# Local and global attention followed by a gated MLP: the order of every engine laid out by a list scheduler in the kernel

## The chip, the cores and the metric

The kernel runs on one core of a Trainium2 chip. The time is device microseconds of that core for one execution, median of several runs. A core has five engines that run side by side, each through its own list of instructions in order: TensorE (PE in the profile; its weight loads are PEld), VectorE (DVE), ScalarE (ACT), GpSimd (POOL) and SyncE (SP). Here POOL issues all loads from memory, which convert fp32 to fp16 on the way, and SP issues the stores and the copies within the on-chip memory. All transfers share 16 DMA engines. An engine whose next instruction waits for something lets everything behind it wait too.

## The reference

There are 8 batches, 8 heads, 512 local and 32 global positions, and a head size of 64. A local query sees the local keys within 32 positions and all 32 global keys; a global query sees all 544 keys. The attention output then goes through two matrix products with a hard-swish between them.

```python
s_g = scale * q_g @ concat(k_g, k_l).T;  out_g = softmax(s_g) @ concat(v_g, v_l)
s_ll = where(|i - j| <= 32, scale * q_l @ k_l.T, -1e9)
s_l = concat(scale * q_l @ k_g.T, s_ll); out_l = softmax(s_l) @ concat(v_g, v_l)
x = concat(out_g, out_l) as 4352 rows (batch, position) of 512 (head, channel)
h = x @ w_in                      # 512 x 2048
g = h * clip(h + 3, 0, 6) / 6
out = g @ w_out                   # 2048 x 512
```

## The kernel before

**Attention of a batch.** `qk_loads` (L85 to L101) loads q and k of a batch as eight transfers of 128 positions by 8 heads by 64 channels, and for every second batch the global q and k of two batches (`qkg`). Four `pair_qk` (L180) turn two heads at a time: eight TensorE transposes into the one `t` buffer of PSUM, then one ACT copy to `qk` (L189). `global_qk` (L169) does it for `qkg`. `v_loads` (L103) loads V into overlapping windows of 96 keys, `spread` (L115) copies the global V beside each window by three DMAs, and `shift` (L121 to L124) makes the two copies of V shifted by 32 and 64 keys by four DMAs inside the on-chip memory; both go through SP.

The batch has six blocks: four local ones of 128 queries (`local_scores` L191, `turn` L220, `local_av` L229, `local_x` L251) and two global ones, for even and odd heads (`global_scores` L262, `turn`, `global_av` L294, then `global_x` L309). A local block is 64 small score matmuls (32 of L206 and 32 of L208), then for each of the 8 heads one DVE instruction that adds the mask and takes the maximum (L214) and one ACT exponential (L217), then 8 transposes (L223), an ACT copy to `et` (L225), 32 matmuls with V (L236), a normalisation on DVE (L248, L249), and a DMA transpose on SP that puts the result in `xt` (L255). PSUM has one buffer each for scores (`s`), transposes (`t`) and attention output (`a`), and three for the MLP (`m`).

**MLP of a batch.** `first` (L318) makes one of 16 slices of the hidden layer: four matmuls into an `m` buffer (L323), an ACT ReLU to `t1` (L327), and on DVE the gate (L328) that also frees the `m` buffer. `second` (L332) makes 128 rows of the output in four quarters of four matmuls (L338), a DVE copy (L342), and a store on SP (L355). In the first batch, `first` runs on two halves of 256 positions.

**What sets the order.** The loop over blocks (L423 on) runs a pipeline of three stages: scores of block i, transposes of block i-1, V matmuls of block i-2. Between the stages `fill` (L385) takes work from the list `pending` (the MLP of earlier batches), 4/3 pieces at a time. The framework then orders the instructions by that priority and by free buffers. The loads of batch b+1 are issued six at a time within the blocks of batch b. At the start POOL issues: q and k of batch 0, the identity, the global q and k, the mask, V, then `w_in` in four transfers and `w_out` in sixteen (L404 to L414); batch 1 follows.

The TensorE list that comes out is periodic from the second batch on. Per batch, with S for local and GS for global scores, T for transposes, A and GA for V matmuls, pair for q and k, F for `first`, W for `second`, and the number of matmuls behind each:

```text
W1 pair8 W5 pair8 W2 GS32 A32 W4 T6 W8 pair8 W5 pair8 W3 S64 GA24 W8 T6 W16 S64 GA24 W4 T8 W8 F8
S64 A32 F4 T8 F8 S6 F4 GX1 S17 F4 S41 A32 F8 T8 F4 GS6 F8 GS2 F4 GS24 A32 F4 T8 F8
```

## Time and profile before

| What | us |
|---|---|
| median of 3 runs (428.4 to 430.57) | 428.52 |
| the profiled execution, its own time | 429.63 |
| its span, first to last instruction | 427.8 |
| outside the span | 1.83 |
| PE busy | 360.1 (84%) |
| ACT busy | 243.5 (57%) |
| DVE busy | 221.2 (52%) |
| POOL busy | 119.6 (28%) |
| bytes moved by DMA | 44.54 MB |

A row of a timeline gives the start in microseconds, how long the merged run of instructions lasts, engine, line, operation, written and read tiles, and how many; in brackets how long the engine stood idle before it and what released it. A row of windows gives a stretch of time, its length, and for each engine its busy time and number of instructions, then the granted TensorE clock (1.00 is full), the DMA share and the rate in GB/s. A matmul's length includes its way through the array, so the pace of a run is read from start to start, not from the single durations.

### The profile page before, as it was taken

How to read it: one execution, taken by the hardware profiler on the slowest of the kernel's cores; microseconds unless marked ns; L12 is line 12 of the kernel's file. 1: busy time of each engine (PE TensorE's matmuls, PEld its weight loads, DVE VectorE, ACT ScalarE, POOL GpSimd, SP SyncE). 2: the span in 40 equal slices, each digit the busy share in tenths (PEclk: the TensorE clock that was granted, in tenths of full speed). 3: DMA queues.
4: the chain of work that ended last, by engine and by line, in shares of the span. 5: the costliest groups of instructions: out<-in, count | busy, mean ns of one | idle time of the engine just before them, and what ended most of it. 6: DMA issues, size and time to landing. Idle time of an engine off the chain costs nothing.

```text
span 427.8 us, 13784 instructions
## 1 busy us (share of the span) xinstructions
PE 360.1 (84%) x5784; PEld 205.1 (48%) x5784; DVE 221.2 (52%) x873; ACT 243.5 (57%) x533; POOL 119.6 (28%) x170
## 2 busy tenths in 40 slices
PE   0447059597999999999989999999999989999996
PEld 0325036365555455555545554555445544544642
DVE  2044015474348734873577357735773578437611
ACT  1456118675567756785677567856676667227500
POOL 8923697473642034203420252010000000000000
PEclk9999999888999999999999999999999999999999
DMA  9999999999999359945993698353602110120021
GB/s 94 107 207 201 141 152 181 141 178 152 112 190 150 41 76 182 157 44 75 183 158 36 82 174 163 33 85 89 136 12 52 52 41 14 51 75 0 2 74 74
DMA packets 140541, 44.54 MB, mean 104 GB/s; under 512 B 125888, under 2 KB 134592, under 8 KB 140480
## 3 DMA queue, kind: packets, MB, share of 16 engines
q0 software_dynamic: 111040, 17.57, 60.0%
q1 hardware_dynamic: 29440, 26.09, 26.9%
q8 instruction: 45, 0.74, 0.7%
q14 instruction: 16, 0.13, 0.1%
HBM read 35.13 MB, written 8.91 MB: 103 GB/s over the span
## 4 chain that ended last, share of the span: by engine, by line
PE 61%; ACT 14%; DMA 8%; issue 6%; POOL 5%; DVE 5%; POOLq 0%; ACTq 0%
PE m L338 27%; PE m L323 19%; ACT t L327 5%; ACT ex L217 5%; DMA win<-in_moe_w_in_dram 4%; DVE gt L328 4%; PE s L281 4%; PE t L186 3%; PE t L223 3%; PE a L236 2%; DMA wout<-in_moe_w_out_dram 2%; PE s L206 2%; ACT qk L189 2%; DMA qn<-in_q_l_dram 1%; POOL kn L101 1%
## 5 line engine op out<-in xcount | busy, mean ns | idle before, releaser
L323 PE MATMUL m<-xt,win 128*128 128x512 f16 (+1 forms) x576 | 129.4, 363 | 21.2 <-DVE gt L328 12.4
L338 PE MATMUL m<-wout,gt 128*128 128x512 f16 x512 | 123.1, 380 | 0.0
L328 DVE SCALAR_TENSOR_TENSOR gt<-t,m 128x512 f16<-128x512 f32 (+1 forms) x144 | 86.8, 625 | 45.4 <-ACT t L327 44.7
L327 ACT ACTIVATE t<-m 128x512 f32<-128x512 f32 (+1 forms) x160 | 82.0, 532 | 42.4 <-PE m L323 41.0
L217 ACT ACTIVATE ex<-sm,mx 128x128 f16<-128x128 f32 x256 | 78.7, 388 | 41.7 <-DVE mx L214 41.6
L323 PEld LDWEIGHTS <-win 128*128 128x128 f16 x640 | 59.5, 99 | 64.2 <-issue 18.7
L214 DVE CUSTOM_DVE_ANT_0 sm<-s,mask 128x128 f32<-128x128 f32 x256 | 57.0, 287 | 48.5 <-PE s L208 41.2
L338 PEld LDWEIGHTS <-gt 128*128 128x128 f16 x512 | 46.7, 98 | 46.2
L111 POOL DMA_DIRECT2D vw<-in_v_l_dram x48 | 35.6, 746 | 98.1 <-PE a L236 86.6
L189 ACT COPY qk<-t 128x1024 f16<-128x1024 f16 x32 | 32.6, 1018 | 49.2 <-PE t L186 49.0
L225 ACT COPY et<-t 128x1024 f16<-128x1024 f16 (+1 forms) x48 | 44.7, 930 | 12.7 <-PE t L223 12.6
L342 DVE COPY ot<-m 128x512 f32<-128x512 f32 x34 | 23.4, 688 | 46.7 <-PE m L338 46.7
L284 DVE TENSOR_REDUCE mx<-s 128x1 f32<-128x768 f32 x16 | 15.3, 958 | 39.7 <-PE s L281 39.7
L186 PE MATMUL t<-ident,qn 128*128 128x128 f16 x128 | 14.3, 233 | 23.2 <-POOL ident masks.py:199 9.6
L101 POOL DMA_DIRECT2D qn<-in_q_l_dram x32 | 29.1, 909 | 16.6 <-PE t L186 13.3
L101 POOL DMA_DIRECT2D kn<-in_k_l_dram x32 | 29.2, 911 | 0.6 <-DMA wout<-in_moe_w_out_dram 0.6
L186 PEld LDWEIGHTS <-qn 128*128 128x128 f16 x128 | 10.8, 104 | 36.7 <-DMA qn<-in_q_l_dram 18.3
L206 PEld LDWEIGHTS <-qk 64*32 64x32 f16 x1024 | 15.7, 90 | 23.8 <-issue 15.9
L206 PE MATMUL s<-gt,qk 64*32 64x32 f16 x1024 | 22.1, 185 | 5.8 <-issue 4.5
L223 PE MATMUL t<-ident,ex 128*128 128x128 f16 x256 | 24.4, 234 | 2.3 <-ACT ex L217 2.2
L236 PE MATMUL a<-vw,et 128*32 128x65 f16 x1024 | 17.0, 202 | 9.1 <-DMA vw<-vw 3.9
L208 PE MATMUL s<-qk 64*32 64x96 f16 x1024 | 23.5, 211 | 0.0
(53 smaller groups left out, 292.6 us busy)
## 6 DMA issues: line engine op xcount, KB each, us to landing
out_dram<-ot SPq DMA_DIRECT2D x32, 256.0 KB, 3.7
vw<-vw SPq DMA_DIRECT2D x16, 330.0 KB, 5.7
vw<-vgs SPq DMA_DIRECT2D x24, 198.0 KB, 4.7
qn<-in_q_l_dram POOLq DMA_DIRECT2D x32, 128.0 KB, 5.4
kn<-in_k_l_dram POOLq DMA_DIRECT2D x32, 128.0 KB, 5.6
vw<-in_v_l_dram POOLq DMA_DIRECT2D x32, 96.0 KB, 4.8
vw<-vw SPq DMA_DIRECT2D x16, 165.0 KB, 5.4
win<-in_moe_w_in_dram POOLq DMA_DIRECT2D x4, 512.0 KB, 15.7
```

What stands on the lines that cost most here:

```text
L101: return [lambda o=o, i=i: nc.gpsimd.dma_start(out=o, in_=i) for o, i in work]
L186: nc.tensor.matmul(out=ps[:, c0:c0 + P], lhsT=nat[:, j, p * P:(p + 1) * P], rhs=ident, is_transpose=True)
L189: nc.scalar.copy(out=dst, in_=ps.rearrange("d (i s) -> d i s", i=2))
L206: nc.tensor.matmul(out=o[:, 0:Sg], lhsT=lhs, rhs=st["gt"][rows, p, gc:gc + Sg])
L214: nc.vector.tensor_tensor_reduce(out=sm, in0=ps[:, h % 2, h // 2, :], in1=m, scale=-scale, scalar=3.0e38, op0=ALU.add, op1=ALU.min, accum_ ...
L217: nc.scalar.activation(out=ex[:, h, :], in_=sm, func=EXP, scale=-1.0, bias=mx)
L223: nc.tensor.matmul(out=ps[:, h * P:(h + 1) * P], lhsT=ex[:, h, :], rhs=ident, is_transpose=True)
L225: nc.scalar.copy(out=et[:, 0:n, :].rearrange("c h q -> c (h q)"), in_=ps)
L323: nc.tensor.matmul(out=ps[:, 0:n], lhsT=w_in_t[c // WC][:, m, c % WC * P:(c % WC + 1) * P], rhs=x[:, m, 0:n], start=(m == 0), stop=(m == N ...
L327: nc.scalar.activation(out=t1[:, 0:n], in_=ps[:, 0:n], func=RELU, bias=0.5, scale=1.0 / 6.0)
L328: nc.vector.scalar_tensor_tensor(out=g[:, 0:n], in0=t1[:, 0:n], scalar=1.0, in1=ps[:, 0:n], op0=ALU.min, op1=ALU.mult)
L338: nc.tensor.matmul(out=ps, lhsT=gs[c][:, t0:t0 + P], rhs=w_out_t[c], start=(c == 0), stop=(c == NDFF - 1))
```

## The change

**Order.** The loop over blocks, `fill` and `pending` are gone. Every piece of work is registered by `op(engine, t, cost, f, deps, ...)` with a priority time `t`, a cost in microseconds, the pieces it depends on and the buffers it takes and frees. `lay_out` replays the five engines and the queue of loads with these costs, picks at each step the ready piece with the smallest `t` on the engine that is free first, and so lists all pieces. They are then emitted in that order, and `tc.manual_schedule()` makes the framework keep it. The maximum and the exponential of each head are pieces of their own (`head_max`, `head_exp`), so that MLP work on ACT and DVE can stand between two heads.

```python
def lay_out():
    ...
    while len(order) < len(ops):
        best = None
        for e, line in avail.items():
            can = [(r, o) for o in line for r in (ready(o),) if r is not None]
            if not can:
                continue
            now = max(free[e], min(r for r, _ in can))
            o = min((o for r, o in can if r <= now), key=lambda o: o.t)
            if best is None or now < best[0]:
                best = (now, e, o)
        ...
        order.append(o)
...
with tc.manual_schedule():
    for o in lay_out():
        o.f()
```

**Loads.** For batches 0 and 1, q and k come as two transfers each of four heads, in which a partition holds four consecutive positions, so that 256 numbers (1 KB) are read in one piece instead of 64. `w_out` comes in four transfers instead of sixteen. POOL issues: global V, q and k of heads 0 to 3, identity, mask, global q and k, q and k of heads 4 to 7, V of batch 0, `w_in`, all of batch 1, `w_out`, then q and k of batch 2. The mask takes two POOL instructions instead of eight, and three DVE copies.

```diff
+        if b < LONG:
+            h = i // 2 * (H // 2)
+            load(st[n].rearrange("p (h c) -> p h c", h=H)[:, h:h + H // 2, :],
+                 src[b, h:h + H // 2].rearrange("h (p t) d -> p h (t d)", t=NT))
...
+    def spread(b, eng=None):
...
+            if b == 0:
+                nc.vector.tensor_copy(out=o, in_=i)
+            else:
+                nc.sync.dma_start(out=o, in_=i)
...
+        cuts = (0, half, NW - 1) if b == 0 else (0, NW - 1)
...
-        dst = qk[b % 2][p].rearrange("d (i c) -> d i c", i=2)[:, :, Sg:Sg + Sl]
-        nc.scalar.copy(out=dst, in_=ps.rearrange("d (i s) -> d i s", i=2))
+        if b < LONG:
+            copy(out=dst.rearrange("d i (s t) -> d i s t", t=NT),
+                 in_=ps.rearrange("d (i t s) -> d i s t", i=2, t=NT))
+        else:
+            copy(out=dst, in_=ps.rearrange("d (i c) -> d i c", i=2))
```

**Batch 0.** Its four pairs use the `t` buffer and the three `m` buffers of PSUM, and their copies alternate between ACT and DVE. For batches 0 and 1 a pair is 16 transposes of 64 columns instead of 8 of 128. The first block's scores are issued per pair. `spread` is three DVE copies of 32 by 3168 numbers; `shift` comes in two halves, and the first local block needs only the first. `x` is turned by four TensorE transposes and a DVE copy instead of the DMA transpose on SP:

```diff
+    def local_x_turn(x):
+        flat = x.rearrange("q i h d -> q (i h d)")
+        ps = t_tile(NP * P)
+        for p in range(NP):
+            nc.tensor.matmul(out=ps[:, p * P:(p + 1) * P], lhsT=flat[:, p * P:(p + 1) * P], rhs=ident,
+                             is_transpose=True)
+        return ps
+    def local_x_copy(b, j, ps):
...
+        nc.vector.tensor_copy(out=st["xt"][:, :, j * P:(j + 1) * P],
+                              in_=ps.rearrange("d (p q) -> d p q", p=NP))
```

**Global scores.** In `global_scores` the loops are exchanged: the four pairs, which write four different groups of 32 PSUM partitions, are now innermost.

```diff
-        for p in range(NP):
...
-            for i in range(NG):
...
-                for c0, n, rhs in parts:
-                    nc.tensor.matmul(out=o[:, i, c0:c0 + n], lhsT=lhs, rhs=rhs)
+        for i in range(NG):
...
+            for c0, n, k0 in parts:
+                for p in range(NP):
+                    g, t = st["gt"][rows, p, :], qk[b % 2][p][rows, :]
+                    nc.tensor.matmul(out=ps[p * Sg:(p + 1) * Sg, i, c0:c0 + n], lhsT=g[:, g0:g0 + Sg],
+                                     rhs=g[:, g0 + Sg:g0 + 2 * Sg] if k0 is None else t[:, k0:k0 + n])
```

**The lists that come out.** TensorE starts like this (xT is the new transpose of `x`, GX the turn of a batch's global result), and the second fence is one batch of its later, periodic part:

```text
pair32 gqk4 S32 pair32 S96 T8 S64 T8 S64 A32 xT4 A32 T8 GS32 xT4 A32 T8 F12 GS32 xT4 A32 F8 T6 F8 xT4 F4
GA24 F4 gqk4 F8 pair16 F12 T6 F12 pair16 F24 GA24 F8 pair16 F12 GX1 pair16 F12 S64 F8 S64 F8 T8 F8 S64 A32
F4 pair8 W12 T8 W12 A32 S64 W4 T8 W8 A32 gqk4 W4 GS32 ...
```

```text
pair8 GS32 W4 T8 W8 GS32 pair8 A32 W4 T6 W8 pair8 GA24 W4 T6 W4 S64 GA24 W4 GX1 F4 W4 F4
S64 T8 F12 A32 F8 S64 F12 T8 F8 A32 F8 S64 F8 W4 pair8 W8 T8 W8 A32 W4
```

The first `pair8` of the third line belongs to batch 2 and stands ahead of the first W. On DVE the three `spread` copies stand ahead of the copy of pair 1. On SP the list is: the two halves of the shift of batch 0, spread and shift of batch 1, spread of batch 2, the transpose of the first block of batch 1, the shift of batch 2, and then stores and transposes in turn. POOL still lets no more than eight loads be under way.

## The prediction, made before the changed kernel was run

> **What bounds the kernel now.** I read the page's slices first, to see where TensorE is idle.

> ```profile
> span 427.8 us, 13784 instructions
> ...
> PE   0447059597999999999989999999999989999996
> ...
> PEclk9999999888999999999999999999999999999999
> DMA  9999999999999359945993698353602110120021
> ```

> A slice is 10.7 us. PE has holes in the first ten slices and is at nine tenths from there to the end, while DMA is full for thirteen. So there are two stages with two questions: what delays PE in the first 105 us, and whether "nine tenths" is really dense. For the first I read the timeline of PE (start, length, engine, line, count, idle time before).

> ```profile
> 50.10 0.37 PE L323 MATMUL m<-xt,win 128*128 128x256 f16 x1 [7.91 <-DMA xt<-x]
> 55.12 0.29 PE L186 MATMUL t<-ident,qn 128*128 128x128 f16 x1 [4.65 <-DMA qn<-in_q_l_dram]
> ...
> 62.95 2.10 PE L323 MATMUL m<-xt,win 128*128 128x256 f16 x9
> ...
> 84.28 0.21 PE L206 MATMUL s<-gt,qk 64*32 64x32 f16 x4 [4.46 <-issue]
> ...
> 85.66 1.89 PE L323 MATMUL m<-xt,win 128*128 128x256 f16 x8
> ...
> 104.99 1.06 PE L338 MATMUL m<-wout,gt 128*128 128x512 f16 x2
> ```

> The MLP could begin at 50.10 and stops after one slice, because the next PE instruction transposes a q of batch 1 whose load POOL issued at 48.51, behind sixteen `w_out` loads. It really begins at 62.95, and the first `second` comes at 104.99. From there the list is periodic, as the windows cut at its repeats show (stretch, length, busy us of PE, PEld, DVE, ACT, POOL, clock, DMA share, GB/s):

> ```profile
> 104.99:148.17 43.18, 41.13 (x702) 22.68 (x701) 25.31 (x101) 27.98 (x61) 16.20 (x22) 0.99 1.17 125
> 148.17:191.30 43.13, 40.93 (x707) 22.73 (x706) 25.86 (x101) 29.44 (x64) 12.03 (x15) 1.00 0.90 114
> ...
> 363.90:427.80 63.90, 59.63 (x415) 30.31 (x412) 28.48 (x53) 19.31 (x39) 0.00 (x0) 0.99 0.14 46
> ```

> The six periods fill 104.99 to 363.90, so 43.15 us each; with the 63.90 of the tail: 105.0 + 258.9 + 63.9 = 427.8. In a period PE idles 43.15 - 40.95 = 2.2 us, ACT is 68% busy and DVE 60%: none is a bound but PE.

> **Steady part.** The MLP's 128 matmuls run at 0.216 us from start to start (96 of them in the last 20.73 us of the chain), 27.7 us; the other 15.5 are attention and waits. Two things in it change.

> ```profile
> 237.81 0.19 PE L281 MATMUL s<-gt 64*32 64x32 f16 x1
> ...
> 238.85 0.44 PE L236 MATMUL a<-vw,et 128*32 128x65 f16 x32
> ...
> 251.69 0.21 PE L206 MATMUL s<-gt,qk 64*32 64x32 f16 x8
> ...
> 252.30 0.37 PE L301 MATMUL a<-vw,et 128*32 128x65 f16 x24
> ...
> 262.83 1.02 PE L323 MATMUL m<-xt,win 128*128 128x512 f16 x4 [0.94 <-DVE gt L328]
> ```

> First, the 32 global score matmuls take 238.85 - 237.81 = 1.04 us, the 64 local ones, whose neighbours write different partition groups, 252.30 - 251.69 = 0.61. In the new loop order neighbours differ as well. Half of 0.61 is 0.3, no change is 1.04; I take 0.45, nearer to the local row because it has the same four groups and somewhat longer rows. Two a batch: 2 x 0.59 = 1.2 us (0 to 1.5).

> Second, waits of F for a free `m` buffer (0.94 here and 0.95 once more in the period): eight exponentials in a row, 2.44 us on ACT, stand before the ReLU that feeds the gate. Between single heads the ReLU waits for one exponential, 0.30. Of the 2.2 us idle I count 1.6 gone (0 to 2.8; the scores split around these waits, S6 and S17, hide up to 0.6 more). New period: 43.15 - 1.2 - 1.6 = 40.3, bounds 39 to 43.15 - 0.6 = 42.5. Six periods: 242.

> Finer mixing could cost changes between large and small matmuls. Eight MLP matmuls from 255.65 to the scores at 257.46 take 1.81 instead of 8 x 0.216 = 1.73, so 0.08 a change, and by the two lists the new period has 23 changes against 24: I add nothing. [...]

> **First work of the MLP.** POOL's first load starts at 1.25. Rows: a 256-packet load 0.60, a 512-packet one 0.77 (`w_in`), V 0.75, identity and two mask instructions about 1.2 with gaps. 1.25 + 0.60 + 2 x 0.77 + 1.2 + 2 x 0.6 + 2 x 0.77 + 6 x 0.75 = 11.8 for the last V. Loads land 4 to 6 us after issue, so pairs 0 and 1 start near 7 (before: the first copy at 12.35), pairs 2 and 3 near 10, and the chain of one `t` buffer and four ACT copies (12.35 to 19.7) becomes two copies on each engine. ACT then has 32 exponentials x 0.305, four `et` copies of 1.0, two pair copies and `gt`: 16 us, ending near 25 with handoffs. V is later: landed near 16, the second half of the shift issued then; before, from SP's first shift at 23.76 to the V matmul at 32.24 took 8.5 us, so 24 (22 if half the bytes take less, 27 if `w_in` slows it). Block 1 needs it, and behind its V matmuls in PE's list stand T, GS and all else. Normalisation 0.9, xT about 0.4, DVE copy 0.6 (L342 has the same 128 by 512 numbers: 0.69), handoffs 0.4: first F near **27** (23 to 32). The DMA transpose that falls away held 37.81 to 50.10. The DVE `spread` has no row: by the memsets (768 halves in 0.38) 1.6 us each, by the fp32 mask copy (128 in 0.23, most of it taken as per element) 3.8; I take 1.6, 4.8 in all, done near 10; even 11.4 ends before V, which covers it. The strided pair copies may cost 1.0 (as L189) to 2.0; V covers those of batch 0.

> **From there to the first W.** Work of ACT in between, by the new list: 32 ReLUs x 0.42, four pair copies x 1.02, two global exponentials x 0.97, two `et` copies x 1.0 and two x 0.79, `gt` 0.3, 17 exponentials x 0.305: 28.5 us; PE needs only about 21 (128 F x 0.11 and 7 of attention). So 27 + 28.5 = 55.5 (60 with doubled copies). But ahead of the first W stands a pair of batch 2, which needs all its q and k, loaded last. In the order of the loads, in fp16 bytes as the page counts them: batch 0 1.55 MB, its shift 1.0, `w_in` 2.1, batch 1 1.55, its spread and shift 1.6, `w_out` 2.1, q and k of batch 2 1.0: 10.9 MB. The trace gives 155 GB/s where 256-byte reads dominate (54 to 66 us) and 201 to 221 where `w_in` and `w_out` do (24 to 42). 2.55 MB at 155 is 16.5 us, 8.35 at 205 is 40.7; with 3 us until the first byte: **60** (50 to 72, the latter at 157 GB/s, the mean from 3 to 50 us now). DMA, not ACT, ends last; PE waits some 5 us.

> After such a wait PE starts slowly. The granted clock reads 0.72 and 0.60 in 80 to 90, behind the 4.46 us wait, and eight L323 matmuls from 85.66 take 1.81, where four from 77.29 take 0.45: with what follows the wait costs about 2 us, which I add. [...]

> At the first W the old list is further: one score block, two V blocks, one global score block and three transposes more, less one pair, 0.6 + 0.7 + 1.0 + 1.35 - 0.45 = 3.2 us that the new one owes.

> **Queues passed.** On SP three transposes of batch 1 stand behind batch 2's shift, which waits for its V: about 67, plus 8.5. Their F follows 64 W and some 6 us of attention after 62, near 82, so 7 us cover it; a V later than that costs one for one. Stores queue there too, with four `ot` buffers to cover them.

> **Tail.** 63.9 less one pair of cheaper global scores and a little waiting: 62.3 (61.5 to 64). The 64 global F are bound by ACT and DVE as before.

> **Sum** against the profiled 427.8: 60 + 2 + 3.2 + 242 + 62.3 = 369.5. Outside the span 1.83, and the median stood 1.1 below the profiled 429.63: about 370.

> **Rivals.** (1) The start moves less than laid out and the mixing does nothing, since the list follows assumed costs, with engines waiting in a fixed order: first W at 72, period 43.15 - 1.2: 72 + 5 + 251.7 + 62.3 + 0.7 = 392. For it: DMA is full for 139 us. Against: PE is busy in only 51 of the first 100 us, and the long waits name loads that stood behind others. (2) DMA keeps pace: q and k of batch 2 are there by 52, ACT's 55 holds, but its copies overlap, W at 52, period 39: 52 + 3 + 234 + 61.5 + 0.7 = 351. For it: 1 KB reads and no pause at 12 to 18 us, where only 47 GB/s flow. (3) Slower: exponentials between ReLUs turn each head into a handoff that holds an `m` buffer. Its price: one exponential and a PE to ACT handoff, 0.30 + 0.27, times 32 heads, 18 us a period, 58 in all: 60 + 5 + 348 + 62 + 0.7 = 476. It decides from a period of 50.5 up (65.2 + 6 x 50.5 + 62.3 = 430), about 0.3 us of PE time lost per head. Against it: ACT is free 11 us in 40 and three `m` buffers lie between. (4) The gains cancel against new waits within 0.5%.

> **Chances.** Forecast, 357 to 382: 0.53. (1), 382 to 415: 0.22. (2), below 357: 0.18. (3): 0.05. (4): 0.02. Faster by over 0.5% 0.93, within 0.5% 0.02, slower 0.05; half a per cent is about what a measurement here can tell from no change. The low end is (2) with the shortest terms, 50 + 3 + 234 + 61.5 = 348.5, the high end (1) with 72 + 5 + 255 + 64 = 396: range 346 to 398.

> **What would show it.** Right: the first F near 27 behind a wait for shifted V; a PE wait before the first `second` for q of batch 2, that W near 60; repeats of 40.3; global scores of 0.45. Wrong: repeats above 42, a first W before 55 or after 70, or PE waiting for `xt` near 82.

## The result and the profile after

The changed kernel takes 387.98 us (median of 4 runs, 381.04 to 390.58) against 428.56 us; the ratio is 0.894, with a 95% interval of 0.883 to 0.904. The ratio leaves out executions more than 1.5% above the fastest of their kernel, so it rests on 381.04 and 385.83 us (mean 383.4), while the profiled execution is the slowest of the four: 390.58 us, with a span of 388.8 us. The kernel is faster, as forecast, and the time lies inside the range of 346 to 398, but 18 us above the forecast of 370 and outside its band of 357 to 382. The numbers below are of the span of 388.8 unless said otherwise; what is said to cost the kernel something is an amount in that execution.

The page's slices of the changed kernel, 9.7 us each:

```profile
span 388.8 us, 13880 instructions
...
PE   2559984969889997999999988999999999999995
...
PEclk9999998687999998999999998999999999999999
DMA  8999999999998299915992599476402102400022
```

TensorE (PE) is busy from the fourth slice on, but for the seventh and the ninth; the wide holes of the kernel before are gone. New is the second row: the granted clock drops from the seventh to the tenth slice and twice later. DMA is still full for thirteen slices.

The windows of the changed kernel, cut at the first W and then at the same place of each period (stretch, length, busy us of PE, PEld, DVE, ACT and POOL with instructions, granted clock, DMA share, GB/s):

```profile
69.50:122.99 53.49, 46.73 (x818) 24.62 (x819) 26.94 (x107) 33.46 (x72) 28.52 (x38) 0.89 1.73 157
122.99:164.84 41.85, 39.30 (x691) 20.54 (x690) 26.40 (x107) 28.19 (x64) 12.05 (x15) 0.96 1.23 125
164.84:203.38 38.54, 38.54 (x702) 20.91 (x701) 25.81 (x100) 28.93 (x63) 12.03 (x15) 1.00 1.07 121
203.38:245.98 42.60, 40.44 (x707) 21.54 (x706) 26.78 (x106) 29.47 (x64) 13.68 (x17) 0.96 1.20 126
245.98:284.52 38.54, 38.54 (x702) 20.91 (x701) 25.86 (x100) 28.94 (x63) 2.21 (x3) 1.00 0.47 93
```

A period of the kernel before took 43.15 us and had 2.2 us in which TensorE stood idle. The third and the fifth row take 38.54 us, with TensorE busy throughout. The second and the fourth take 3.3 and 4.1 us more, at a clock of 0.96. The first period takes 53.5.

What stands in these longer rows is shown by the timeline of PE:

```profile
33.45 2.76 PE L393 MATMUL m<-xt,win 128*128 128x256 f16 x12
...
63.56 0.23 PE L215 MATMUL t<-ident,qn 128*128 128x128 f16 x1 [1.93 <-DMA qn<-in_q_l_dram]
66.86 0.29 PE L215 MATMUL t<-ident,qn 128*128 128x128 f16 x1 [2.10 <-DMA qn<-in_q_l_dram]
69.50 5.28 PE L409 MATMUL m<-wout,gt 128*128 128x512 f16 x12
86.00 0.37 PE L194 MATMUL t<-ident,qkg 128*128 128x128 f16 x2 [3.47 <-issue]
...
153.57 0.23 PE L243 MATMUL s<-gt,qk 64*32 64x32 f16 x7 [2.55 <-issue]
153.92 4.03 PE L393 MATMUL m<-xt,win 128*128 128x512 f16 x12
...
234.38 0.21 PE L243 MATMUL s<-gt,qk 64*32 64x32 f16 x8 [2.16 <-issue]
```

Three things are to be seen. Ahead of the first W, at 69.50, TensorE waits for q and k of batch 2, as the prediction had it. Twelve W then take 5.28 us where 12 x 0.216 = 2.6 is their pace: half the clock. And at 86.00, 153.57 and 234.38 TensorE stands for 2.2 to 3.5 us with "issue" as the releaser: no semaphore, so neither data nor a buffer was missing. At 117.02 there is one more of 1.99 us; the trace names a DVE maximum for it, which the F behind it does not use, and the packets and instruction counts below put it with the others. The prediction had no such term.

### The profile page after: what moved, and what is told of

It is laid out like the page before. It is cut to its first block, busy times and chain, and to the rows that moved or that the text cites. A ratio compares the mean times of both kernels' runs of the same rounds, so it can differ in the third digit from the quotient of the medians.

```text
span 388.8 us, 13880 instructions
## 1 busy us (share of the span) xinstructions
PE 347.0 (89%) x5868; PEld 193.7 (50%) x5868; DVE 231.7 (60%) x885; ACT 242.1 (62%) x532; POOL 105.9 (27%) x144
## 3 DMA queue, kind: packets, MB, share of 16 engines
q0 software_dynamic: 98432, 17.57, 62.9%
## 4 chain that ended last, share of the span: by engine, by line
PE 72%; DMA 14%; POOL 5%; DVE 4%; issue 3%; ACT 1%; POOLq 0%
PE m L409 30%; PE m L393 26%; DMA kn<-in_k_l_dram 7%; DMA wout<-in_moe_w_out_dram 5%; PE t L263 4%; PE t L215 2%; PE a L279 2%; DMA xt<-x 2%; PE s L243 2%; PE s L337 2%; POOL vw L86 2%; PE s L245 2%; DVE gt L404 1%; PE a L364 1%; POOL win L86 1%
## 5 line engine op out<-in xcount | busy, mean ns | idle before, releaser
L409 PE MATMUL m<-wout,gt 128*128 128x512 f16 x512 | 128.4, 390 | 0.0
L258 ACT ACTIVATE ex<-sm,mx 128x128 f16<-128x128 f32 x256 | 88.2, 398 | 24.6 <-DVE mx L252 24.3
L252 DVE CUSTOM_DVE_ANT_0 sm<-s,mask 128x128 f32<-128x128 f32 x256 | 60.5, 285 | 17.4 <-PE s L245 14.9
L86 POOL DMA_DIRECT2D qn<-in_q_l_dram x28 | 24.5, 885 | 81.3 <-PE t L215 72.5
L225 ACT COPY qk<-t 128x1024 f16<-128x1024 f16 x24 | 24.2, 1010 | 32.2 <-PE t L215 32.2
L294 DVE RECIPROCAL rec<-a 128x8 f32<-128x8 f32 (+1 forms) x48 | 9.1, 190 | 42.1 <-PE a L279 22.2
L86 POOL DMA_DIRECT2D kn<-in_k_l_dram x28 | 24.8, 893 | 9.3 <-DMA qn<-in_q_l_dram 4.2
L354 ACT ACTIVATE eg<-s,nm 128x480 f16<-128x480 f32 (+1 forms) x32 | 13.9, 487 | 15.2 <-DVE nm L345 11.4
L295 DVE TENSOR_TENSOR x<-a,rec 128x512 f16<-128x512 f32 x32 | 22.1, 691 | 1.1
L263 PEld LDWEIGHTS <-ex 128*128 128x128 f16 x256 | 18.1, 104 | 7.3 <-issue 1.5
```

Source lines behind the costliest of these rows:

```text
L86: nc.gpsimd.dma_start(out=o, in_=i)
L225: copy(out=dst, in_=ps.rearrange("d (i c) -> d i c", i=2))
L252: nc.vector.tensor_tensor_reduce(out=sm, in0=ps[:, h % 2, h // 2, :], in1=m, scale=-scale, scalar=3.0e38, op0=ALU.add, op1=ALU.min, accum_ ...
L258: nc.scalar.activation(out=ex[:, h, :], in_=sm, func=EXP, scale=-1.0, bias=mx)
L263: nc.tensor.matmul(out=ps[:, h * P:(h + 1) * P], lhsT=ex[:, h, :], rhs=ident, is_transpose=True)
L409: nc.tensor.matmul(out=ps, lhsT=gs[c][:, t0:t0 + P], rhs=w_out_t[c // WC][:, c % WC, :], start=(c == 0), stop=(c == NDFF - 1))
```

## The experiments

Each run was timed beside the kernel before on the same chip (its medians there: 429.6 to 430.2 us). Unless the edit says otherwise, all else is as in the changed kernel; the list scheduler moves a few pieces in answer to an edit.

### Taking the loads away, and putting them back for nobody

```diff
-    LONG = 2
+    LONG = 8
...
-        for i, nat in enumerate((st["qn"], st["kn"])):
+        for i, nat in enumerate((state[b % 2]["qn"], state[b % 2]["kn"])):
...
-            qk_load_ops(n, t)
+            for key in ("qkload", "v", "vhalf", "spread"):
+                made[n][key] = made[n - 2][key]
```

> Edit: as the run with 1 KB reads for all batches, but batches 2 to 7 load nothing: they turn the q and k of batches 0 and 1 again and use their V, so six eighths of the output are those of the first two batches' data; all computing instructions stay. Theory A: no wait ahead of the first W (-8, -2.5 of half pace), none of TensorE's stalls without a semaphore after the first 80 us (-12 to -15 with the half clock behind each), all periods near 38.5 + 0.45: the time is 358 to 366. Rival C (these stalls belong to the computing itself, not to the loads): the stalls at about 86, 117, 153 and 234 us stay, each with its half clock, and the time is 374 to 380.

Measured: 367.09 us (366.05 to 368.06), ratio 0.854 (0.851 to 0.856). The slices of the run without loads:

```profile
span 363.7 us, 14017 instructions
...
PE   2548998999999999999999999999999999999995
...
PEclk9999999999999999999999999999999999999999
DMA  7999994220103110211011102210022101200032
```

After the seventh slice nothing is left of the holes, and the clock stays at full speed to the end. After the "issue" stall at 26.62 there is only one more, of 0.2 us. So theory A holds, though the time lies 1 us above its range, and rival C falls: the stalls go with the loads. TensorE had 24 pairs x 0.11 = 2.6 us more of transposes in this run; against 388.8 the loads therefore cost 388.8 - 363.7 + 2.6 = 27.7 us of the profiled execution. From the trace of the changed kernel these are 10.2 us of stalls without a semaphore (3.47 + 1.99 + 2.55 + 2.16), 6.2 of waits for q and k of batch 2, 1.3 for xt, and the half clock, whose records overlap TensorE's work at 69.5 to 74.6, 86.0 to 91.7, 153.6 to 156.5 and 235.0 to 238.4: 17.1 us at half pace lose 8.6. Together 26.3. Against the 383.4 us of the two executions behind the ratio the same subtraction, 383.4 - 367.1 + 2.6, gives 18.9; only the profiled one can be taken apart.

What are the stalls? The list of DMA queues on the page of the changed kernel has a queue that no line of the kernel uses:

```profile
q0 software_dynamic: 98432, 17.57, 62.9%
q1 hardware_dynamic: 26896, 24.96, 29.8%
q8 instruction: 46, 0.75, 0.9%
```

It moved 46 packets of 16 KB, and TensorE ran 5,868 matmuls and 5,868 weight loads: 255 instructions a packet. In the trace's packet records, beside TensorE's instructions (packets counted from 0; "ahead" is the number of instructions that TensorE had begun when the packet started, less 256 for each earlier packet):

```text
packet   start     end  ahead   next TensorE instruction at
     8   82.95   84.50    449    86.00   after 3.47 us
     9   91.56   92.74    295    92.79
    12  114.22  115.74    434   117.02   after 1.99 us
    17  150.68  152.07    410   153.57   after 2.55 us
    20  171.74  172.91    189   173.05
    23  195.42  196.31    402   196.35
    28  231.59  232.94    384   234.38   after 2.16 us
    35  278.57  279.94    178   279.97
```

Most packets start when TensorE is some 150 to 300 instructions on. Where a packet starts at 384 or later, TensorE stands still until 1.3 to 1.5 us after the packet's end (in other runs this also follows packets that started at 320 to 380); packet 23, at 402, found TensorE in large matmuls, where instructions are used up slowly (8 begun in its 0.89 us), and cost nothing. In the run without loads no packet after 60 us starts later than 313. A count shows it more sharply: at the end of all five stalls (26.04, 86.00, 117.02, 153.57, 234.38) TensorE had begun 449 or 450 instructions past 256 for each packet before the one that had just ended. The 256 a packet comes from these counts themselves: 6,912 instructions from 26.04 to 234.38, over 27 packets. In the thirteen traces that can be read this holds for 52 of the 53 idle times of at least 0.5 us with "issue" as the releaser, in both kernels and in every order. So the stalls are TensorE running out of instructions, because its own 16 KB come late. The dense stretches are the scores: a block of 64 is 128 instructions in 0.6 us.

Whether the loads alone do it, or only the waits that come with them, is asked by loading into tiles that nothing waits for.

```diff
+            for i in range(4):
+                load_op(t + 0.1 * i, 2048, 256, lambda n=n, i=i: idle_qk_load(n, i), made[n - 2]["av"][0:1])
...
+        if j == 0 and "dq" in st:
+            nc.tensor.matmul(out=ps[0:D, 0, 0, 0:D], lhsT=st["dq"][:, 0:D], rhs=st["dk"][:, 0:D], start=True, stop=True)
```

> Edit: the run without loads for batches 2 to 7, with their loads of q, k and V (256-byte reads, 22 loads a batch) put back, but into tiles that nothing waits for: one spare matmul of each batch, whose result is overwritten, reads them long after they have landed, so that the next loads start in step with TensorE. TensorE's list is that of the run without loads but for two matmuls of 64 rows a batch; the output is still six eighths of the first two batches' data. Theory A (loads crowd out the 16 KB packets of the queue marked instruction): TensorE stalls of 2 to 4 us with no semaphore named come back while the loads run, each at the end of a late packet, with a granted clock below 1.00 behind them, and the time rises from 367 to 372 to 384. Rival C (TensorE's losses came from waits for data and what these did to the order): no such stall after the first 60 us and 366 to 369.

Measured: 371.7 us (371.22 to 372.48), ratio 0.864 (0.860 to 0.868), which is 4.6 us more than without loads; the intervals do not meet. PE's timeline of this run:

```profile
60.54 0.19 PE L264 MATMUL s<-gt,qk 64*32 64x32 f16 x3 [1.16 <-issue]
...
81.91 0.32 PE L302 MATMUL a<-vw,et 128*32 128x65 f16 x17 [2.06 <-issue]
87.80 1.89 PE L419 MATMUL m<-xt,win 128*128 128x512 f16 x8 [0.86 <-issue]
```

Stalls come back where the loads are dense, with nobody waiting for data: these three and one of 0.76 us at 74.34 make 4.8 us, about what the time grew, and the first period grows from 41.55 to 45.77. But the two later ones do not come back, and the granted clock stays at 1.00. Theory A is right in kind and too high in size (its range began at 372), and it had a lower clock behind the stalls, which did not come. This run also lacks the copies of V inside the on-chip memory (1.6 MB a batch), so of the 18.9 or 27.7 us some 4.6 are the loads' traffic by itself, and the rest needs the waits, the copies, or both; these two were not told apart.

### Moving the wait

The first edit keeps batch 2's turns from standing ahead of the first W:

```diff
+            if b == 2:
+                need = need + second_of[0, 3][1:2]
```

> Edit: the four turns of batch 2's q and k may start only after the first two W tiles. Theory A (TensorE's list held it): the 8 us in which TensorE waits for batch 2's q and k ahead of the first W in the changed kernel, and about 2.5 us of half pace behind it, go; first W near 61 and the time near 378, 10 below the changed kernel's 388. Rival B (the transfers are late as a whole): TensorE waits for the same bytes a few us later, at the turns themselves, at V or at xt, and the time stays at 386 to 389.

Measured: 385.13 us (381.46 to 386.36), ratio 0.895 (0.891 to 0.898), not to be told from the changed kernel. The first W comes at 63.91 instead of 69.50; one period later 2.7 of these 5.6 us are left (120.30 against 122.99). PE's timeline and two windows of this run:

```profile
67.57 0.38 PE L194 MATMUL t<-ident,qkg 128*128 128x128 f16 x4 [1.75 <-DMA qkg<-in_k_g_dram]
80.28 0.27 PE L215 MATMUL t<-ident,qn 128*128 128x128 f16 x2 [2.00 <-DMA qn<-in_q_l_dram]
88.40 0.21 PE L279 MATMUL a<-vw,et 128*32 128x65 f16 x2 [2.62 <-issue]
```

```profile
63.91:120.30 56.39, 46.20 (x827) 24.70 (x825) 29.60 (x122) 35.13 (x77) 29.79 (x40) 0.92 1.93 157
120.30:162.46 42.16, 39.60 (x691) 20.55 (x689) 26.40 (x107) 28.20 (x64) 12.04 (x15) 0.96 1.34 120
```

By its time this is nearly rival B (386 to 389), by its mechanism neither theory. The waits for q and k, 6.2 us in the changed kernel, are gone, and one of 1.75 us for the global q and k is left. The row at 80.28 names a load of q, but the q that this turn reads had landed at 63.9, and all q and k of batch 2 at 66.2; the load that landed at 79.86 is batch 3's. This idle time ends 1.69 us after the end of an instruction packet, at 449 instructions, and the one at 88.40 ends 1.28 us after one, at 449 too. So stalls without a semaphore took the place of the wait: 2.48 us before the first W, at 62.05, then these two, then 2.26 and 2.56 us at 112.78 and 150.88.

The second edit reads q and k of all batches in pieces of 1 KB (LONG = 8, nothing else).

> Edit: q and k of all batches are read in pieces of 1 KB as those of batches 0 and 1. This takes some 49,000 of 125,000 DMA packets away and none of the bytes; each later pair becomes 16 transposes of 64 columns instead of 8 of 128 (0.57 against 0.46 us by the rows of the changed kernel: 24 x 0.11 = 2.6 us more on TensorE). Theory A (the 256-byte reads crowd the DMA engines, so q and k of batch 2 and the 16 KB packets on the queue marked instruction are late): the wait ahead of the first W falls from 8 us to under 3, TensorE's unexplained stalls of 2 to 3.5 us become fewer than four, and the time falls to 372 to 381. Rival B (bytes, not packets, set the pace of the loads): the wait and the stalls stay and the time is 388 to 391.

Measured: 385.33 us (382.78 to 388.54), ratio 0.895 (0.892 to 0.899). The second period falls to 38.44, but the first is 54.30 and the first W stands at 70.48. POOL's timeline and TensorE's in this run:

```profile
43.70 0.78 POOL L86 DMA_DIRECT2D qn<-in_q_l_dram  x1
...
46.62 0.75 POOL L86 DMA_DIRECT2D kn<-in_k_l_dram  x1 [0.66 <-DMA vw<-in_v_l_dram]
```

```profile
63.25 0.64 PE L211 MATMUL t<-ident,qn 128*64 128x128 f16 x8 [8.61 <-DMA qn<-in_q_l_dram]
```

All q and k of batch 2 are issued by 47.4, where the changed kernel issued its last at 62.9, and still TensorE waits to 63.25. They landed at 63.2 to 67.2, against 63.5 to 69.4. Neither theory's range holds the time. At the start the bytes ahead, `w_out` and batch 1, set the time, as rival B has it. TensorE still has five stalls of 1.4 to 3.8 us, so fewer packets of loads do not remove them. The five further periods take 196.5 us instead of 200.1, but 197.3 in the run before, whose packets are those of the changed kernel: a gain from fewer packets is not shown.

The third edit takes traffic away instead: global V beside the windows by DVE for all batches.

```diff
-            if b == 0:
-                nc.vector.tensor_copy(out=o, in_=i)
-            else:
-                nc.sync.dma_start(out=o, in_=i)
+            nc.vector.tensor_copy(out=o, in_=i)
```

> Edit: the global V is copied beside the windows by DVE (three copies) for every batch, not only for the first; the three DMAs of SP for it, 0.6 MB a batch, go. DVE gets 3 x 1.2 = 3.6 us more a batch, by the row of these copies in the changed kernel. Theory A (TensorE's stalls and late loads come from the load on the DMA engines in the first 120 us): 1.8 MB fewer before 120 us at about 150 GB/s is 12 us of DMA time, the first periods shorten and the time is 376 to 384. Rival (the copies stand before gates on DVE and TensorE waits for them, or the DMA engines are not what is short): 386 to 396.

Measured: 383.25 us (five of six executions 380.65 to 384.05), ratio 0.889 (0.885 to 0.892); theory A's range, at its upper end, but the interval lies inside the changed kernel's, so a gain is not shown. The profiled execution ran at a granted clock of 0.58 and took 568.11 us, so this run has no trace that can be read.

The fourth edit undoes what the change did for batch 0's x and V:

```diff
-        if b == 0:
+        if b < 0:
             turned = op(PE, t + 3.6, 0.23, lambda: h.update(t=local_x_turn(h["x"])), [norm], takes=("t",),
```

> Edit: in the changed kernel, batch 0's x goes into xt by the DMA transposes on SP and its global V beside the windows by SP's DMAs, as for the other batches; its pairs keep their four buffers. Theory A (the first F decides what follows): the first F moves from 33.5 to 42 to 48, the first W by as much, and the time is 394 to 402. Rival B (up to 120 us the loads set the pace, whatever TensorE has done by then): the first F is as late, but the time rises by less than 4, 385 to 392.

Measured: 386.05 us (383.15 to 388.81), ratio 0.898 (0.893 to 0.902). The first F comes at 39.36, less late than theory A had it, and the first W at 70.86; the time is that of the changed kernel: rival B. But the list moved more than the edit asked: batch 2's turns now stand behind the first W (their last k lands at 72.24), as in the first edit's run, and a stall of 2.98 us without a semaphore, ending at 69.47, stands ahead of it. Against that run the first F comes 5.0 us later, the first W 7.0, and the time is still the same. Batch 0's shorter way to its first F earns nothing that these runs can tell.

The same question put to the kernel before, batch 1's loads ahead of `w_out`:

```diff
+    loads = qk_loads(1) + v_loads(1)
+    for f in loads:
+        f()
```

> Edit: the kernel before with the loads of batch 1 issued before the sixteen of w_out instead of after them. Theory A (at the start TensorE waits behind turns of batch 1's q whose loads stand behind w_out): its stop from 50.7 to 62.95 goes, the first W, at 104.99, comes 8 to 12 us earlier, and the time is 416 to 421. Rival B (bytes pace the start, so a new order only moves the wait): 426 to 430.

Measured: 424.89 us (421.73 to 429.33), ratio 0.984 (0.978 to 0.990): between the two. The stop at 50.7 goes, but now the first F itself waits:

```profile
71.20 2.74 PE L323 MATMUL m<-xt,win 128*128 128x256 f16 x12 [8.61 <-DMA xt<-x]
```

Its xt comes from four transposes on SP that now start at 55.21, behind batch 1's copies of V, where before they ran from 37.81 to 50.10. The first W moves from 104.99 to 101.56 only.

So the largest gain of the change, the first W at 69.5 instead of 105.0, is not explained by single parts: undoing batch 0's ways moves it by 1.4 us (7.0 against the run whose turns stand alike), the order of the loads in the kernel before by 3.4. The order of the engines at the start and the 1 KB reads of batches 0 and 1 were not undone by themselves.

### The period

Global scores with the old loops in the changed kernel:

```diff
-            for c0, n, k0 in parts:
-                for p in range(NP):
+        for p in range(NP):
+            for i in range(NG):
...
```

> Edit: the changed kernel with the loops of the global scores as they were (pairs outermost); the order of all engines stays. The changed kernel's trace has 0.47 us for 32 of these matmuls, the old one 1.04, 16 groups a run. Theory (TensorE is the bound, so all of it counts): 16 x 0.57 = 9 us more, 397. Rival (half of it or more lies beside waits for the maximum behind it): 388 to 392.

Measured: 392.19 us (389.05 to 393.43), ratio 0.911 (0.908 to 0.915). An undisturbed period of this run:

```profile
161.00:200.71 39.71, 39.71 (x703) 22.09 (x701) 25.88 (x100) 28.95 (x63) 12.03 (x15) 1.00 1.16 111
```

39.71 - 38.54 = 1.17 a period, all of it in the scores (2.10 instead of 0.95 us for the two groups): the theory. The total rose by 4 us between the medians and by 7.6 by the ratios, whose intervals leave room for some 3 to 12; 9 were expected, so the total does not decide. In the profiled execution the stalls were shorter (1.18 instead of 2.55 us in the second period), which gives part of it back. Its start is that of the changed kernel but for these loops, and its first W comes at 67.38, with 3.4 us of waits for q and k instead of 6.2.

The same loops alone, put into the kernel before:

> Edit: the kernel before with only the loops of the global scores exchanged. Theory (TensorE is the bound and does 32 of them in 0.47 instead of 1.04 us): 16 x 0.57 = 9 us less, 419 to 420. Rival (the kernel before waits for the maximum or for gates behind them, so that a faster score run only makes a wait longer): 424 to 429.

Measured: 423.4 us (422.01 to 424.49), ratio 0.983 (0.979 to 0.988). Two windows of this run:

```profile
101.79:147.79 46.00, 41.45 (x703) 22.11 (x702) 25.43 (x101) 28.89 (x63) 17.39 (x24) 0.96 1.48 131
189.82:231.87 42.05, 39.69 (x703) 21.23 (x702) 25.93 (x101) 28.98 (x63) 12.03 (x15) 1.00 0.97 117
```

43.15 became 42.05 where nothing disturbs, nearly as the theory has it; the total lies between the two. The first window gave 2.8 us back to a stall of 2.38 us at 107.95, again without a semaphore.

The exponentials of a block in one piece again:

```diff
-            exps.append(op(ACT, t + 0.05 + i * dt + lag, 0.292, ex, [mx] + exps[0:1],
-                           takes=("ex",) if i == 0 else (), ends=(("sm", mx),)))
...
+        e_all = op(ACT, t + 0.05 + lag + 3 * dt, 0.292 * H, all_exps, mxs, takes=("ex",),
+                   ends=tuple(("sm", mx) for mx in mxs))
+        exps = [e_all]
```

> Edit: in the changed kernel, the eight exponentials of a local block are one piece of work again, so that ACT does them in a row after all eight maxima; the list scheduler is the same and moves its other pieces a little. Theory (mixing single heads with ReLUs removed TensorE's waits for gates): the period of 38.5 grows by the 1.4 to 2.2 us of waits that the kernel before had in it, 8 x 1.8 = 14: time 396 to 406. Rival (the scheduler's order of the pieces is what counts, not their size): 386 to 390.

Measured: 390.56 us (388.81 to 392.07), ratio 0.907 (0.903 to 0.910). By the total alone this would be near the rival (by the ratios it is 5.6 us above the changed kernel, where 14 were expected); the windows and the timeline say otherwise:

```profile
160.08:201.09 41.01, 39.24 (x710) 21.38 (x710) 26.10 (x102) 29.71 (x64) 12.04 (x15) 1.00 1.11 120
201.09:241.53 40.44, 38.66 (x697) 20.63 (x697) 26.14 (x102) 28.24 (x63) 13.68 (x17) 1.00 1.20 125
```

```profile
193.74 1.89 PE L393 MATMUL m<-xt,win 128*128 128x512 f16 x8 [0.98 <-DVE gt L404]
```

TensorE idles 1.8 us a period again, with the old wait for a gate, and the periods are 40.4 to 41.0 instead of 38.5. That is the theory, 1.9 to 2.5 us a period. In the total it is partly hidden: this order has one long stall (2.79 us at 85.78) and one of 1.02 us where the changed kernel's profile has four of 2 to 3.5 us. Two effects of opposite sign need two readings; a total gives one.

### A version that keeps both gains

All three edits of the start for all batches:

> Edit: three edits of earlier runs together in the changed kernel: batch 2's turns only after the first two W tiles, reads of 1 KB for q and k of all batches, and the global V copied by DVE for all batches. It removes some 49,000 of 125,000 packets, and with the 21 copies of the global V 4.2 MB of DMA traffic; TensorE gets 2.6 us more of transposes and DVE 3.6 us a batch. Theory A (the load on the DMA engines up to 120 us is what the kernel loses to, and only together do the edits lower it far enough): first W near 62, two or three stalls of TensorE without a semaphore instead of four, 373 to 379. Rival B (wait and stalls only change their place): 381 to 386, as each edit alone.

Measured: 384.1 us (383.68 to 387.02), ratio 0.894 (0.890 to 0.898): rival B's range, but for another reason than it gave. The same W that stands at 164.84 in the changed kernel came at 156.83; then three periods took 40.5 to 40.9:

```profile
238.22:279.14 40.92, 39.78 (x750) 21.28 (x749) 28.69 (x107) 29.59 (x65) 2.20 (x3) 1.00 0.35 72
```

Against the undisturbed 38.54 that is 6.7 us more in the three, since TensorE now idles 1.14 us a period for the `et` copy on ACT and has more transposes. The profile of the changed kernel loses 4.1 us to a stall and the half clock behind it in the same stretch, so at the end the two spans still differ by 6.6 (382.2 against 388.8); by the ratios the two kernels are the same. The last run keeps the edits to the batches whose loads crowd the start:

```diff
-    LONG = 2
+    LONG = 4
...
-            if b == 0:
+            if b < 4:
                 nc.vector.tensor_copy(out=o, in_=i)
...
+            m["spread"] = [op(DVE, t_spread + 0.5 * c, 1.25, lambda c=c: spread(b, [c]), [vg] + vs + free_v)
+                           for c in range(3)]
...
+            if b == 2:
+                need = need + second_of[0, 3][1:2]
```

> Edit: the three edits of the run before, confined to the stretch in which the loads fill the DMA engines: reads of 1 KB for q and k and the global V copied by DVE only for batches 0 to 3 (the copies of batches 1 to 3 as three separate pieces), batch 2's turns after the first two W tiles; from the third period on TensorE's list is that of the changed kernel. Theory (the start of the run with all three edits is 8 us shorter at the same W, 156.83 against 164.84, and it gave them back by periods of 40.2 to 40.9 instead of 38.5): both gains together, 374 to 381. Rival (in every order the gain is eaten by other stalls, as in the single edits): 382 to 387.

Measured: 377.11 us (375.56 to 378.7), ratio 0.877 (0.874 to 0.879), below the changed kernel's whole interval and within the theory's range. Its windows:

```profile
66.83:114.28 47.45, 44.86 (x872) 23.84 (x871) 30.58 (x113) 33.67 (x74) 22.11 (x30) 0.95 1.36 145
114.28:152.59 38.31, 38.18 (x706) 20.29 (x705) 28.20 (x106) 27.77 (x64) 12.63 (x16) 1.00 1.25 130
152.59:192.21 39.62, 38.65 (x703) 20.84 (x702) 25.93 (x100) 28.97 (x63) 12.04 (x15) 1.00 1.29 124
192.21:230.98 38.77, 38.77 (x706) 21.25 (x705) 26.31 (x104) 29.25 (x64) 13.69 (x17) 1.00 1.24 123
```

The first period is 6 us shorter than in the changed kernel, and the later ones have almost no stall. One wait of 5.71 us remains, for the global q and k of batches 2 and 3, up to 66.45.

## Why the prediction was right, and where it was not

**The direction** was right, and so were the two waits it named: TensorE waited for loads that stood behind others, and for gates behind exponentials; both kinds of wait shrank. The size was not: the time lies in the band of rival 1 (382 to 415), because a term is missing and the way to the first W came out long. The sum of 369.5 and the span of 388.8 compare by stages (the kernel before cut at the same W; the last column is the run without loads, its 2.6 us of extra transposes left in):

| Stage | Before | Predicted | Measured | Without loads |
|---|---|---|---|---|
| to the first W | 105.0 | 60 | 69.5 | 61.1 |
| first period, with slowed clock and owed work | 43.4 | 45.5 | 53.5 | 41.6 |
| five further periods | 215.6 | 201.5 | 200.1 | 195.6 |
| from the last period's end | 63.8 | 62.3 | 65.7 | 65.5 |

**First F near 27**: 33.45. V did hold the first local block, to 23.66, as said, though TensorE stood only 0.35 us for it; behind it came a stall of 2.04 us without a semaphore and, in TensorE's list, a turn, global scores and a second V block, which the sum named but put at nothing. The late F cost nothing that shows in the time: in the run that undoes batch 0's ways it comes 5.9 us later still.

**First W at 60, set by DMA**: the wait was for q and k of batch 2, as said, and the time lay in the bounds of 50 to 72. The 55.5 for ACT's work was too low: without later loads the first W comes at 61.06. The loads put 8.4 us on top of that, 6.2 of them waits. The last k of batch 2 landed at 69.37; from 3 us to there the DMA engines moved 174 GB/s, 11.6 MB, against the 155 and 205 that I mixed to 191 for 10.9 MB. The bytes were 6% more than summed and the rate lay between the forecast's and that of my upper bound (157, 72 us). That POOL issued the last q and k late was not the cause: the run with 1 KB reads issued them 16 us earlier, and its first W was no earlier. Nor was a load there 4 to 6 us after its issue, as before: these q and k took 7 to 20 us.

**Steady term, 40.3**: the average of the five periods is 40.0, but the agreement is an accident of two errors. The undisturbed period is 38.54. The global scores gave 1.15 as costed (1.2; 0.47 us against my 0.45). The waits gave 3.45 instead of 1.6: all 2.2 of idle time went, and 1.25 more with it. Part of that is in the scores, which the list no longer splits around the MLP (S6, S17, S41): from start to start, the idle time in them taken off, the local ones take 2.46 instead of some 2.9 us a period, and the global ones, by the run with the old loops, would take 2.10 instead of 2.37. Mixing single heads holds about 2.2 of the 3.45, by the run with the exponentials in one piece. (By the two lists the old period has 26 changes between large and small matmuls, not 24; the new one has 23, so that nothing was to be added either way.) Rival 3 is thereby settled: the handoffs cost nothing, and mixing gains.

**The term that was missing** is the stalls without a semaphore: 10.2 us, and 6 of the 8.6 at half clock, behind them. The step that failed is that the sum put the time in which TensorE waits for its own instructions at nothing. The profile before had it, 4.46 us at 84.28 and 3.14 us in this row:

```profile
101.16 0.28 PE L236 MATMUL a<-vw,et 128*32 128x65 f16 x12 [3.14 <-issue]
```

I read the first only for the clock behind it and did not ask why it stood there. The queue marked "instruction" shows it: both end at 449 instructions past the earlier packets, too. The wait before the first W did cost what I gave it for the clock: 2.7 us (5.28 against 2.6) for 2.

**Tail, 62.3**: 65.7. Its cut stands at another place of the list: behind it 494 matmul records follow, 415 before, so part of the 3.2 us that I placed in the first period belongs here.

**Rival 2** (DMA keeps pace, 351) falls with the first W. **Rival 1** gave nearly the right time, 392, and was half right: the start did move less than laid out (its 72 against 69.5), but the mixing does work, and its period of 42 is wrong. That its time is nearer than mine is luck: it had no stalls either.

**Signs**: of those that would show me wrong, repeats above 42 came once (42.60, with a stall in it) and a first W after 70 nearly (69.5); of the signs of being right, the global scores came (0.47), the wait for q came, the first F and the repeats did not; for `xt` TensorE waited 1.12 us at 100.45, not near 82.

## What to carry to other kernels

Look up an engine's idle time that names no semaphore before costing a change: here, where TensorE ran many small matmuls beside heavy DMA traffic, its own instructions came late, and a denser order did not cure that by itself (7.6 us in two stalls before, 10.2 in four after). When a change makes every engine denser, ask which queue now has to deliver sooner, and cost it at the rate that the slices show for that mix of loads. Where a total hardly moves, compare undisturbed periods: with the exponentials in one piece, a loss of 2 us a period and fewer stalls lay on top of each other. And check a releaser that the profile names against the time at which that data landed.

## What the runs showed of the hardware

**The clock fell after some short waits.** Half pace followed waits of 1.90 us (at 99.72, the run with all three edits), 2.16 and 2.55 us, but not those of 1.99 us (at 117.02) and 2.06 us (the run with idle loads, at 81.91). The clock records of the changed kernel show half pace for 3.4 us twice (153.1 to 156.5, 235.0 to 238.4), for 6.8 us (84.8 to 91.7) and for 10.2 us (64.4 to 74.6). From which wait on the clock falls is not shown: these waits do not order by length.
